# One queue for the first loads, three homes for raw weights and more idle products at the start of a fused RWKV-6 and MLP kernel

## The chip, the cores and the metric

The kernel runs on one core of a Trainium2 chip. Times are microseconds of device time for one execution; the kernel is called once with all its inputs in HBM and leaves its output in HBM. A shorter time is better.

The engines are called by the names of the profile: PE is TensorE (PEld its weight loads), DVE is VectorE, ACT is ScalarE, POOL is GpSimd and SP is SyncE, which here only issues DMA transfers.

## The reference

Two blocks, one after the other. The first is a linear recurrence over 768 time steps for 4 batches and 8 heads of 48 values; the second is a layer norm and an MLP with a residual.

```python
B, H, S, D = r.shape                      # 4, 8, 768, 48
state = zeros((B, H, D, D))
for t in range(S):
    kt, vt, rt, wt = k[:, :, t], v[:, :, t], r[:, :, t], w[:, :, t]
    cur = einsum('bhd,bhe->bhde', u[None] * kt, vt)
    y[:, :, t] = einsum('bhd,bhde->bhe', rt, state + cur)
    state = wt[..., None] * state + einsum('bhd,bhe->bhde', kt, vt)

x = y.transpose(0, 2, 1, 3).reshape(B, S, H * D)          # (4, 768, 384)
mu, var = mean(x), mean((x - mu) ** 2)                    # over the last axis
xn = (x - mu) / sqrt(var + 1e-6) * g_ln
out = x + maximum(xn @ w_ch1, 0) @ w_ch2                  # 384 -> 1536 -> 384
```

All inputs and the output are float32.

## The kernel before

The work is cut into eight rounds (4 batches, 2 halves of 384 time steps each), and each round into two units of four heads. Round `rnd` has the units `q = 2 * rnd` and `q = 2 * rnd + 1`; in the text "w0" or "k1" means the tile of w or k of unit 0 or 1 of round 0. Time is worked in chunks of 64 steps with six levels of doubling inside a chunk.

A round has a front and an MLP.

- The front (`front`, line 1165) loads w, k and r (`load`, line 350, tiles called `nat`), turns them with PE transposes into PSUM (`turn`, line 380: products `w_ps`, `k_ps`, `r_ps` with the identity) and copies them out on ACT (tiles `w`, `k`, `r`). `totals` (line 421) forms products of w over 2, 4, ... 64 steps (`tot`, `decay`). For each of the six levels `quads` (line 517) multiplies k by r on PE (PSUM tile `a`), `grow` (line 546) scales k and r in place by `tot` on DVE, and `keep` (line 567) writes the masked result to `A`. `own` (line 450) forms the term with u (tiles `rk`, `own_row`), `load_v` (line 649) and `own_term` (line 673, tile `vo`) bring in v, `states` and `outputs` (lines 688 and 752) form the state and the output of the round, `normalize` (line 813) does the layer norm (tile `xn`) and `turn_x` (line 865) turns its result (`xT_ps`, then `xf` on ACT).
- The MLP (`mlp`, line 1055) multiplies `xf` by the first weights (PSUM `h_ps`, in later rounds also `hd_ps`) and the result `h` by the second weights `w_sb` (PSUM `o`), adds the residual and stores.

The MLP weights come in as 24 tiles, called `raw`, of 128 by 384 values in 64-bit words that hold them (384 KB each). `convert` (line 926) fetches one (SP) and rebuilds float32 words from it with three ACT operations (`upper`, `lower`, `sign`) and two DVE operations (`shift`, `join`). The first twelve make the first weights (shown as `w` in the profile, next to the tile `w` of the front), the other twelve make `w_sb`. Later rounds, from round 1 on (`THREE`, line 339), split `xf` into a high and a low part and a difference, tiles `hl` and `xd`; these use the homes of `raw` as well.

**Order.** Nothing is ordered by hand. Each step is an operation of a planner (`Plan`, line 51) with an engine, a cost, the tiles it reads and writes, a priority `pri` (lower first) and, for a DMA, a latency `lat` and a `size` in microseconds of DMA time. `order` (line 104) simulates the engines and writes out one program order for each. A tile has a tag, and a tag has a number of homes, buffers that its tiles take in turn (`HOMES`, line 254). An operation that makes a tile starts, in the plan, when a home is free. DMA transfers are taken by the planner to follow one another: `dma = max(dma, t) + size`, and the data is there at `dma + lat`.

Instructions are then issued in that order on each engine[...].

**Idle products.** Where PE would stand for over 0.4 us before 90 us of planned time, `order` puts in products of zeros (`idle`, line 1241, PSUM tile `idle`), `n` of them with 128 columns each, up to three in one product. The planner's cost of one is 0.24 us, doubled for `t < 5.0`. PE counts as free from 1.0 us of planned time on, SP from 0.8, ACT from 0.9 (`busy`, line 1250).

**The first loads.** In round 0 `front` issues w, k and r of both units: unit 0's three on SP's queue, unit 1's three on ACT's queue, each one transfer of 288 KB; SP's queue then has the broadcast of u (`u_bc`, 192 KB), raw weights, v, and the loads of round 1.

Of the kernel before, what the change touches and what calls it, by code (L numbers as in the profile page):

```python
# [10 lines left out]
F32R = mybir.dt.float32r  # L11
# [39 lines left out]
class Plan:  # L51
# [52 lines left out]
    def order(self, busy, idle=None, until=0.0):  # L104
        ops = self.ops
        left, users, last = {}, {}, {}
        for op in ops:
            left[op.i] = len(op.need)
            for j in op.need:
                ops[j].next.append(op.i)  # L110
            for n in op.uses:
                users[n] = users.get(n, 0) + 1
        free = dict(busy)
        held = {"DVE": 0.0, "POOL": 0.0}
        portless = {"DVE": 0.0, "POOL": 0.0}
        ready = {e: [] for e in free}
        for op in ops:
            if not left[op.i]:
                for e in op.costs:
                    ready[e].append(op)  # L120
        dma, todo, out, tiled = 0.0, len(ops), [], False

        def start_of(op, e):
            t = max(free[e], op.ready)
            tags = [tag for tag, _ in op.new]
            for tag in set(tags):
                n = tags.count(tag)
                if len(self.homes[tag]) < n:
                    return None
                if tag not in self.dynamic and self.queue[tag][0] != op.i:  # L130
                    return None
                t = max(t, sorted(self.homes[tag])[n - 1][0])
            if op.port:
                t = max(t, held["POOL" if e == "DVE" else "DVE"])
                if e == "POOL" and t < op.ready + self.PATIENCE:

                    if portless["DVE"] - t < 0.6 * op.costs[e]:
                        t = max(t, free["DVE"] + 0.3)
            return t

        while todo:
            best = None
            for e, waiting in ready.items():
                at = [(t, op) for op in waiting if (t := start_of(op, e)) is not None]
                if not at:
                    continue
                first = min(t for t, _ in at)
                t, op = min(
                    ((t, op) for t, op in at if t <= first + self.WAIT[e]),
                    key=lambda x: (  # L150
                        x[1].pri + self.STAY * (e == "PE" and x[1].tiled != tiled), x[1].i
                    ),
                )
                if best is None or t < best[0]:
                    best = t, op, e
            assert best
            t, op, e = best
            if idle and e == "PE" and t < until and t - free["PE"] > 0.4 and self.homes[idle[0]]:
                n = int((t - free["PE"]) / (idle[1] * (2 if t < 5.0 else 1)))
                home = min(self.homes[idle[0]])  # L160
                if n and home[0] <= free["PE"]:
                    out.append((free["PE"], lambda n=n, home=home: idle[2](n, home[1])))
                    self.homes[idle[0]].remove(home)
                    self.homes[idle[0]].append((t, home[1]))
            if e == "PE" and op.tiled != tiled:
                tiled = op.tiled
                t += self.DRAIN[tiled]
            for x in op.costs:
                ready[x].remove(op)
            op.eng, op.start, cost = e, t, op.costs[e]  # L170
            free[e] = t + cost
            if e in held:
                (held if op.port else portless)[e] = t + cost
            op.end = t + cost + op.lat
            if op.size:
                dma = max(dma, t) + op.size
                op.end = max(op.end, dma + op.lat)
            for tag, name in op.new:
                home = min(self.homes[tag])
                self.homes[tag].remove(home)  # L180
                self.queue[tag].remove(op.i)
                self.place[name] = home[1]
            for n in op.uses:
                users[n] -= 1
                last[n] = max(last.get(n, 0.0), op.end)
                if not users[n]:
                    self.homes[self.tile_tag[n]].append((last[n] + self.HOP, self.place[n]))
            for j in op.next:
                nxt = ops[j]
                hop = self.HOP if set(nxt.costs) != {e} else 0.0  # L190
                nxt.ready = max(nxt.ready, op.end + hop)
                left[j] -= 1
                if not left[j]:
                    for x in nxt.costs:
                        ready[x].append(nxt)
            fn = op.fn
            out.append((t, fn if len(op.costs) == 1 else lambda fn=fn, e=e: fn(e)))
            todo -= 1
        return [fn for _, fn in out]
# [5 lines left out]
def kernel(  # L205
# [13 lines left out]
    PE, ACT, DVE, POOL, SP = (  # L219
        InOrder(tc, e) for e in (nc.tensor, nc.scalar, nc.vector, nc.gpsimd, nc.sync)  # L220
    )

    B, H, S, D = r.shape
    P = 128
# [5 lines left out]
    U = H // NH  # L230
    TT = 3
    RN = TT * P
# [21 lines left out]
    HOMES = {  # L254
        "nat": 5, "w": 1, "k": 2, "r": 2, "tot": 1, "decay": 3, "rk": 2, "own": 2, "own_row": 1,
        "v": 2, "vx": 2, "vo": 2, "s": 2, "last": 4, "rx": 2, "sx": 2, "x": 2, "xn": 3,
        "xf": 3, "stats": 2, "mv": 2, "rstd": 2, "raw": 4, "rest": 8, "h": 12, "w1": 4, "wl": 4,
    }
    plan = Plan(HOMES | {"a": 2, "b": 4}, ("a", "b"))
    tiles = {}  # L260

    def tile_(tag, name, shape, dtype=F32):
        if name in tiles:
            return tiles[name]
        if tag == "a":
            tiles[name] = a_homes[plan.place[name]]
            return tiles[name]
        if tag == "nat":
            tiles[name] = nat_homes[plan.place[name]]
            return tiles[name]  # L270
        pool = banks if tag == "b" else homes
        t = pool.tile(shape, dtype, tag=f"{tag}{plan.place[name]}", name=name)
        tiles[name] = t
        return t
# [9 lines left out]
    ROWS, ROW = 2, TT * D  # L284
# [62 lines left out]

    SRC = {"w": w, "k": k, "r": r}

    def load(nm, q, eng="SP", pri=None):  # L350
        b, f, g = units[q]
        name = f"nat_{nm}{q}"

        queue = SP if eng == "SP" else ACT

        def go():
            to = tile_("nat", name, None)
            if q // U < ROWS:
                queue.dma_start(
                    out=to[:, 0 : NH * ROW].rearrange("p (h x) -> p h x", h=NH),  # L360
                    in_=SRC[nm][b, ts(g, NH), ds(f * RN, RN)]
                    .rearrange("h (p c) d -> p h (c d)", p=P),
                )
                return
            for c in range(TT):
                queue.dma_start(
                    out=by_tile(to)[:, c, :, 0:D],
                    in_=SRC[nm][b, ts(g, NH), ds(f * RN + c * P, P)].rearrange("h p d -> p h d"),
                )

        if pri is None:
            pri = at(q // U, "wrk".index(nm))
        new = [] if nm == "r" and q in both_units else [("nat", name)]
        cost, size = (0.5, 0.8) if q // U < ROWS else (1.65, 1.2)
        plan.add(eng, cost, go, w=[name], new=new, pri=pri, lat=2.0, size=size)

    def by_tile(t):
        return t.rearrange("p (c h d) -> p c h d", c=TT, h=NH)
# [486 lines left out]
    def turn_x(rnd, kc):  # L865
        ps, xf, pri = f"xT_ps{rnd}_{kc}", f"xf{rnd}_{kc}", at(rnd, 28)
# [12 lines left out]
        hl, xd = f"xhl{rnd}_{kc}", f"xd{rnd}" if kc < 2 else f"xd2{rnd}"  # L879
        new = [("b", ps), ("xf", xf)]  # L880
        if rnd >= THREE:
            new += [("raw", xd)] if kc == 0 else [("rest", xd)] if kc == 2 else []
            new += [("raw", hl)]
        plan.add(
            "PE", 0.33, go, r=[f"xn{rnd}_{i}" for i in range(TT)], w=[ps], new=new,
            pri=pri, lat=0.17,
# [4 lines left out]

        def high():
            if kc < 2:
                tile_("raw", xd, [P, 2, RN], F32R)
            else:
                tile_("rest", xd, [P, RN], F32R)
            tile_("raw", hl, [P, 2, RN], F32R)
            ACT.activation(out=x_parts(rnd, kc)[0], in_=tiles[xf], func=AF.Copy, scale=TOP)
# [266 lines left out]
    def front(rnd):  # L1165
        qs = [U * rnd + g for g in both_units]
        if rnd:
            for q in qs:
                load("w", q)
                load("k", q)  # L1170
        else:
            for i, nm in enumerate("wkr"):
                for q, eng in zip(qs, ("SP", "ACT")):
                    load(nm, q, eng, i)
        if rnd == 0:
            plan.add(
                "SP", 0.6, lambda: SP.dma_start(
# [105 lines left out]
```

## Time and profile before

| what | us |
|---|---|
| median of 7 runs | 556.52 |
| lowest and highest of the 7 | 553.68, 564.84 |
| the profiled execution's own time | 554.24 |
| its span in the profile | 552.5 |
| PE busy in it | 534.4 (97%) |
| DVE busy | 360.0 (65%) |
| ACT busy | 254.6 (46%) |

How to read the lines shown later: an instruction's row names the engine, the operation and its tiles as out<-in, without buffer numbers. "L40" stands in every row, because each instruction is recorded in one helper at that line, so instructions are told apart by their tiles. The chain that ended last is followed back from the last instruction: at each step to what released it, or to the instruction before it on its engine. In a timeline, brackets give the idle time of the engine before the row and what ended it. A product in float32 appears as two instructions, a transpose as one. Idle products count as busy time of PE.

### The profile page before, as it was taken

To read this page: it belongs to the slowest core of one execution; us is meant where nothing else is said; L and a number is where in the kernel's file an instruction comes from. 1 tells how busy PE (TensorE), PEld (TensorE's weight loads), DVE (VectorE), ACT (ScalarE), POOL (GpSimd) and SP (SyncE) were. 2 spreads that over 40 slices of the span, in tenths; PEclk is the share of its full clock that TensorE was granted. 3 is DMA by queue.
4 is the path that set the end of the run, shared out by engine and by line. 5 is a ranking of instruction groups with operands and counts; after the bars stand their busy time and mean duration, and the time that the engine had idled before them with its cause. 6 is when DMAs were issued, how large, how long until landed. Compare 5 with 4: busy or idle time off the path is not lost.

```text
span 552.5 us, 20001 instructions
## 1 busy us (share of the span) xinstructions
PE 534.4 (97%) x8820; PEld 414.2 (75%) x8820; DVE 360.0 (65%) x719; ACT 254.6 (46%) x555; POOL 71.4 (13%) x93
## 2 busy tenths in 40 slices
PE   8998998999999899999999999999999999999997
PEld 7876566666888676889758986798668867967964
DVE  5899999889999876688815987186635422531300
ACT  4788886643384360654605544153245412521500
POOL 7034013371213210011000100000001000000000
PEclk9999999999999999999999999999999999999999
DMA  9975873278534533266005530234003302301101
GB/s 278 260 189 116 247 180 69 74 148 220 146 68 96 139 66 71 68 144 162 30 15 134 105 97 17 70 74 127 17 30 96 110 14 72 112 34 61 40 0 43
DMA packets 118838, 55.80 MB, mean 101 GB/s; under 512 B 86880, under 2 KB 115680, under 8 KB 118752
## 3 DMA queue, kind: packets, MB, share of 16 engines
q1 hardware_dynamic: 117168, 53.65, 38.1%
q8 instruction: 69, 1.13, 0.9%
q10 hardware_dynamic: 1584, 0.88, 0.5%
q14 instruction: 17, 0.14, 0.1%
HBM read 45.05 MB, written 7.10 MB: 94 GB/s over the span
## 4 chain that ended last, share of the span: by engine, by line
PE 86%; DVE 4%; DMA 4%; issue 3%; SPq 1%; ACT 1%; POOL 0%; DVEq 0%; POOLq 0%
PE o L40 33%; PE h_ps L40 17%; PE a L40 17%; PE hd_ps L40 7%; PE w_ps L40 3%; PE k_ps L40 2%; PE r_ps L40 2%; PE kn_ps L40 2%; PE idle L40 2%; DVE A L40 1%; PE xT_ps L40 1%; SPq L40 1%; DMA nat<-in_w_dram 1%; DVE r L40 1%; DVE k L40 1%
## 5 line engine op out<-in xcount | busy, mean ns | idle before, releaser
L40 PE MATMUL o<-w_sb,h 128*128 128x384 f32 x576 | 196.4, 491 | 0.0
L40 PEld LDWEIGHTS o<-w_sb,h 128*128 128x128 f32 x576 | 106.9, 190 | 64.5 <-issue 0.3
L40 ACT COPY h<-hd_ps 128x384 f32<-128x384 f32 x84 | 39.9, 479 | 97.4 <-PE hd_ps L40 96.0
L40 PEld LDWEIGHTS a<-r,k 48*32 48x32 f32 (+5 forms) x4608 | 63.4, 126 | 23.8 <-issue 11.1
L40 DVE SCALAR_TENSOR_TENSOR h<-h_ps,h 128x384 f32<-128x384 f32 x84 | 46.5, 557 | 51.4 <-PE h_ps L40 49.9
L40 ACT ACTIVATE h<-h 128x384 f32<-128x384 f32 x84 | 43.8, 525 | 71.3 <-DVE h L40 70.9
L40 PE MATMUL a<-r,k 48*32 48x32 f32 (+5 forms) x4608 | 69.6, 212 | 6.7 <-issue 4.2
L40 DVE TENSOR_TENSOR x<-o,x 128x384 f32<-128x384 f32 x24 | 13.4, 557 | 79.1 <-PE o L40 79.1
L40 PE MATMUL h_ps<-xhl,wl 128*128 128x384 f32 x252 | 62.4, 356 | 0.0
L40 PE MATMUL h_ps<-xhl,wh 128*128 128x384 f32 x252 | 57.7, 337 | 0.0
L40 PE MATMUL hd_ps<-xd,d 128*128 128x384 f32 x252 | 56.4, 353 | 0.0
L40 DVE TENSOR_TENSOR k<-k,tot 112x768 f32<-112x768 f32 (+1 forms) x45 | 41.2, 915 | 21.9 <-PE a L40 15.8
L40 PEld LDWEIGHTS h_ps<-xhl,wl 128*128 128x128 f32 x252 | 44.1, 188 | 3.3 <-ACT r L40 0.2
L40 PEld LDWEIGHTS h_ps<-xhl,wh 128*128 128x128 f32 x252 | 45.2, 188 | 0.0
L40 PEld LDWEIGHTS hd_ps<-xd,d 128*128 128x128 f32 x252 | 43.2, 188 | 2.6
L40 DVE TENSOR_TENSOR r<-r,tot 112x768 f32<-112x768 f32 (+1 forms) x45 | 41.3, 917 | 0.0
L40 DVE COPY_PREDICATED A<-mask,a 128x768 f32<-128x768 int8 x32 | 38.4, 1207 | 2.5 <-PE a L40 2.5
L40 POOL TENSOR_TENSOR vo<-v,own 128x576 f32<-128x576 f32 x11 | 16.3, 1483 | 152.1 <-DVE x L40 136.7
L40 POOL TENSOR_TENSOR rk<-nat,nat 128x576 f32<-128x576 f32 x11 | 17.5, 1595 | 110.3 <-DMA nat<-in_r_dram 48.3
L40 ACT COPY A<-a 32x384 f32<-32x384 f32 x32 | 15.0, 468 | 27.5 <-PE a L40 27.2
L40 PE MATMUL a<-v,A 64*64 64x48 f32 x384 | 24.4, 221 | 2.7 <-issue 1.2
L40 PEld LDWEIGHTS a<-v,A 64*64 64x64 f32 x384 | 21.2, 133 | 6.9 <-issue 3.5
(94 smaller groups left out, 758.7 us busy)
## 6 DMA issues: line engine op xcount, KB each, us to landing
d<-w1d SPq DMA_DIRECT2D x84, 192.0 KB, 2.5
raw<-in_moe_w_ch_dram SPq DMA_DIRECT2D x24, 384.0 KB, 4.3
v<-in_v_dram SPq DMA_DIRECT2D x48, 96.0 KB, 3.0
out_dram<-x SPq DMA_DIRECT2D x24, 192.0 KB, 1.9
nat<-in_w_dram SPq DMA_DIRECT2D x36, 96.0 KB, 3.0
nat<-in_k_dram SPq DMA_DIRECT2D x36, 96.0 KB, 3.6
nat<-in_r_dram SPq DMA_DIRECT2D x36, 96.0 KB, 2.9
vx<-v SPq DMA_DIRECT2D x32, 72.0 KB, 3.2
```

Of the source, the lines that this page charges most:

```text
L40: return lambda *args, **kw: self.tc.keep_in_program_order(f(*args, **kw))
```

## The change

There are five edits.

- `load` has no engine any more: every load of w, k and r is issued by SP. In round 0 the six loads go in the order w0, w1, k0, r0, k1, r1 with priorities 0, 0.5, 1, 1.5, 2, 2.5, ahead of u's broadcast (priority 5) and of the raw weights (14 and up).
- The planner's figures for a load of w, k or r become 2.2 for the latency (all rounds) and 0.95 for the size (rounds 0 and 1).
- The tag `raw` has three homes instead of four.
- The tile `xd` (kc 0 and 1) has a tag and a home of its own, of the size of one raw home.
- The planner takes 1.78 times 0.24 us instead of 2 times 0.24 for an idle product that is placed before 5.0 us.

```diff
-                n = int((t - free["PE"]) / (idle[1] * (2 if t < 5.0 else 1)))
+                n = int((t - free["PE"]) / (idle[1] * (1.78 if t < 5.0 else 1)))
...
-        "xf": 3, "stats": 2, "mv": 2, "rstd": 2, "raw": 4, "rest": 8, "h": 12, "w1": 4, "wl": 4,
+        "xf": 3, "stats": 2, "mv": 2, "rstd": 2, "raw": 3, "xd": 1, "rest": 8, "h": 12, "w1": 4, "wl": 4,
...
-    def load(nm, q, eng="SP", pri=None):
+    def load(nm, q, pri=None):
...
-        queue = SP if eng == "SP" else ACT
...
-                queue.dma_start(
+                SP.dma_start(
...
-        cost, size = (0.5, 0.8) if q // U < ROWS else (1.65, 1.2)
-        plan.add(eng, cost, go, w=[name], new=new, pri=pri, lat=2.0, size=size)
+        cost, size = (0.5, 0.95) if q // U < ROWS else (1.65, 1.2)
+        plan.add("SP", cost, go, w=[name], new=new, pri=pri, lat=2.2, size=size)
...
-            new += [("raw", xd)] if kc == 0 else [("rest", xd)] if kc == 2 else []
+            new += [("xd", xd)] if kc == 0 else [("rest", xd)] if kc == 2 else []
             new += [("raw", hl)]
...
-                tile_("raw", xd, [P, 2, RN], F32R)
+                tile_("xd", xd, [P, 2, RN], F32R)
...
-            for i, nm in enumerate("wkr"):
-                for q, eng in zip(qs, ("SP", "ACT")):
-                    load(nm, q, eng, i)
+            for i, (nm, q) in enumerate((("w", 0), ("w", 1), ("k", 0), ("r", 0), ("k", 1), ("r", 1))):
+                load(nm, q, i / 2)
```

More of the change, by code (lines that the diff above doesn't have):

```diff
@@ L365, in go @@
             for c in range(TT):
-                queue.dma_start(
+                SP.dma_start(
                     out=by_tile(to)[:, c, :, 0:D],
```

## The prediction

> **What bounds the kernel now.** I read the engine shares first, then the chain that ended last, then the opening microseconds as a timeline, then who waits for whom.
>
> The shares (engine, busy us, share of the span, instructions):
>
> ```profile
> PE 534.4 (97%) x8820; PEld 414.2 (75%) x8820; DVE 360.0 (65%) x719; ACT 254.6 (46%) x555; POOL 71.4 (13%) x93
> ```
>
> PE is the bound, but the figure counts idle products too. The table by stretches splits the span (us, then busy us of PE, PEld, DVE, ACT, POOL, clock, DMA share, GB/s):
>
> ```profile
> 15.00:60.00 45.00, 41.78 (x1090) 32.19 (x1088) 40.87 (x91) 37.55 (x80) 10.99 (x11) 1.00 0.76 198
> 60.00:90.00 30.00, 27.85 (x470) 18.89 (x469) 27.05 (x43) 24.13 (x53) 6.45 (x5) 1.00 0.77 185
> 90.00:552.50 462.50, 451.62 (x7190) 351.84 (x7188) 283.00 (x572) 186.33 (x412) 44.22 (x41) 1.00 0.32 81
> ```
>
> From 90 us on PE has 11 us of holes in 462, and nothing in this change adds or removes a product there. Up to about 57 us, where round 0's MLP begins, PE waits for a serial front: 5.4 us of idle products before 30 us and 9.5 us between 30 and 60. DVE is busy 40.9 of 45 us there. So the span is "when the front of round 0 is finished" plus a nearly solid block of products. A microsecond taken off the front comes off the end, unless another wait takes its place.
>
> The chain at its beginning (start us, us, what):
>
> ```profile
> 0.81 3.42 DMA nat<-in_w_dram
> 4.22 0.14 issue
> 4.36 5.34 PE w_ps L40 x24
> 9.70 1.07 PE k_ps L40 x6
> 10.77 0.66 PE r_ps L40 x6
> 11.42 1.97 PE k_ps L40 x18
> 13.38 1.97 PE r_ps L40 x18
> 15.35 1.51 PE a L40 x96
> ```
>
> Six transposes take 5.34/4 = 1.33 us for w, then 1.07, then 0.66: from about 10.45 us on PE runs the same instruction twice as fast. One k_ps product's duration falls from 418 ns to 272 ns at that point. The granted-clock column says 1.00 throughout, so it doesn't show this. PE's first instructions by time:
>
> ```profile
> 0.99 2.50 PE L40 MATMUL idle<-nought 128*128 128x384 f32 x4 [0.99 <-DVE eps L40]
> 4.36 5.34 PE L40 MATMUL w_ps<-ident,nat 128*112 128x128 f32 x24 [0.87 <-DMA nat<-in_w_dram]
> ```
>
> Idle products ran from 0.99 to 3.49, then PE stood 0.87 us until the first w tile landed.
>
> [...] between 3 and 4 us the ACT queue had 69% and the SP queue 43% of the engines' time, while w of unit 0 was still unfinished. [...]
>
> **The change, part by part.**
>
> *One queue.* ACT loses three DMA issues (0.42, 0.52, 0.53 us), made at 1.00 to 2.54 when it had only a table load and a square root; its first copy comes at 5.89, so this gives nothing; POOL issues no transfer. SP gains three of about 0.55 us: u_bc's issue moves from 2.40 to about 4.05, the first raw weight from 3.13 to 4.75, v from 8.37 to 9 to 10. All of these have slack: ACT first touches a raw weight at 15.76 and v is first read near 39. u_bc is needed at 13.65, which becomes about 11.8; behind six loads of 0.295 MB at the 350 GB/s of the 3 to 6 us stretch it ends near 2.5 + 1.97/0.35 = 8.1. Cost 0; if u_bc came as late as 13, DVE would stand 1 us and lose half of the gain. The w tile of unit 0 no longer shares: 0.16 MB had moved by 3.0, the other 0.135 takes 0.39 at 350 GB/s[...]: 3.6 instead of 4.22. The others follow every 0.84 us: w1 4.5, k0 5.3, r0 6.2, k1 7.0, r1 7.9.
>
> *Idle products.* The planner's w arrives at 0.8 + 0.95 + 2.2 + 0.1 hop = 4.05 instead of 0.8 + 0.8 + 2.0 + 0.1 = 3.7. With PE free at 1.0, n = int(3.05/(0.24 × 1.78)) = 7 columns of 128 instead of int(2.7/0.48) = 5. Five took 2.50 us with the last one's latency, (2.50 - 0.36)/5 = 0.43 each. Seven end their issue at 0.99 + 7 × 0.43 = 4.0. PE then has w (landed 3.6) without a hole, and starts 0.36 us sooner. If w still landed at 4.22, the hole is about 0.2 us and the start is unchanged.
>
> *Clock.* [...] Transposes from 4.0: (7.04 - 4.0)/0.222 = 13.7 slow ones, the other 58.3 at 0.1095 = 6.4 us, ready at 13.43 instead of 15.35. Gain **1.9 us**. [...] Low end 0 if the array isn't released by zero products[...]. The loads stay ahead: w1's transposes start at 6.7, k0's at 8.3, r0's at 9.6, all over 2 us after landing.
>
> *What follows.* DVE's chain starts with `tot<-w` at 10.24, after the fourth copy of w. Copies now end near 8.8; DVE does 4.9 us of products (to 13.7) and meets the first `k<-k,w` at 14.4 instead of 16.31. From there DVE is nearly solid, so the 1.9 us is carried to `xf` at 56.22, where the MLP begins.
>
> *Three raw homes.* Before, four weights are fetched at once; ACT holds one for about 0.54 + 2 × 0.60 = 1.74 us. No ACT wait on a raw transfer appears in the list of waits. With three, the fourth load waits for ACT's first conversion. One home turns in 0.45 issue + landing + 1.74; landing is 5.3 us at the median of the first 40 us and 3.6 from 40 to 90. Three homes thus give one weight in (0.45 + 5.3 + 1.74)/3 = 2.5 us, later 1.93. The kernel uses twelve in 15.8 to 54.6 (3.2 each) and twelve in 54.4 to 85 (2.5 each). I take 0: between 85 and the last `o` group that needs w2 (about 101) lie 16 us. Bounds: from -1 (fewer early weights leave ACT and DVE to the front) to +6, the rival below.
>
> *A home for xd.* Same bytes: four homes of 3,072 per partition before, three and one now. The hl tiles of one round are all released by the same last h_ps product, with xd just earlier, so nobody waits longer. 0.
>
> *New order.* The planner recomputes every engine's order from the new latencies. That is a real uncertainty. The visible piece is here:
>
> ```profile
> 44.06 3.89 DVE L40 TENSOR_TENSOR vo<-v,own 128x576 f32<-128x576 f32 x1
> 47.88 0.54 DVE L40 CUSTOM_DVE_ANT_0 w<-w,held 128x768 uint16<-128x768 uint16 x1
> ```
>
> The same vo takes 0.75 elsewhere; POOL was in rk from 43.00 to 47.34. 3.1 us of DVE's chain stand still.
>
> **Sum.** -0.36 - 1.5 + 0 + 0 = -1.9 us. The profiled execution took 554.24 (span 552.5 and 1.74 around it), so 552.3 against itself. The median of the seven is 556.52, 2.3 higher; the gain applied to that gives 554.6, and I give the number on the median's footing.
>
> **Rivals.**
>
> *A, head start alone: 42%, 554.6, own range 553.0 to 556.2.* For it: DVE's solid front, PE's solid rest.
>
> *B, head start and the block goes: 30%.* If the new order parts rk and vo, 1.9 + 3.1 = 5.0, so 551.5. For it: before, chip time lags the plan by 3.7 us at the first level (15.35 against 3.7 + 72 × 0.11 = 11.6 by the planner's costs), so operations meant to be apart can meet; now 13.43 stands against 12.0. Against: POOL and DVE lag together.
>
> *C, no earlier release: 10%, 556.2.* [...] w may land late and reopen the hole. [...]
>
> *D, raw weights arrive late: 18%, 559.1 to 561.4.* [...] The planner takes 1.05 + 2.0 = 3.05 us for a raw load; landing was 5.3 early. With four homes the extra load ahead hid the 2.25 us difference; with three, an ACT conversion can stand in front of copies that free PSUM, and SP's next loads of k and r stand behind a raw load that waits for its home. Two or three stands of 2.25 us on the front, 4.5 to 6.8, on top of 554.6. It decides once landings of raw loads stay over 3 × 2.53 - 0.45 - 1.74 = 5.4 us. For it: 5.3 is close to that. Against: traffic falls after 40 us, and SP's longest wait on ACT's release was 2.7.
>
> **How the numbers follow.** A measurement of this kernel tells about 0.5% from no change, 2.8 us: the bands end at 553.7 and 559.3. A puts 13 points below and 29 within; B 28 below, 2 within; C 2 below, 8 within; D 2 within, 16 above. Faster 43%, same 41%, slower 16%. The range 549.8 to 559.2 leaves out the far end of B and most of D.
>
> **What will show it.** The page after should have PE without a hole from 1.0 us, the first w_ps at 3.9 to 4.1, transposes falling to 109 ns at or before 7.8, and the first `a` at 13 to 14. `tot<-w` should start near 8.8 and `xf` near 54.3. An ACT row waiting for the raw transfers, or k_ps or r_ps waiting for their loads by over 1 us, means D. A vo on DVE of 0.75 in round 0 means B. I am wrong if the first `a` comes at 13.4 and `xf` still at 56: then the front is held by a transfer or a conversion that I call hidden.

## The result and the profile after

The changed kernel takes **562.27 us** at the median (556.39 to 566.50) against 556.29 for the kernel before on the same chips: a ratio of **1.0095, interval 1.0073 to 1.0116**, so 0.95% slower. The ratios leave out the executions that lie over 1.5% above the fastest of their kernel, so they aren't the quotients of the medians. The forecast was 554.6 with a range up to 559.2. The profiled execution took 559.89 (before: 554.24), its span 557.8 (before: 552.5): 5.3 us longer, close to what the medians say.

The page's line of engine shares, after (engine, busy us, share of the span, instructions):

```profile
PE 538.7 (97%) x8828; PEld 417.8 (75%) x8828; DVE 358.9 (64%) x719; ACT 254.6 (46%) x555; POOL 76.6 (14%) x93
```

PE is busy 4.3 us longer, with eight instructions more. The same stretches as before (us, then busy us of PE, PEld, DVE, ACT, POOL, clock, DMA share, GB/s):

```profile
15.00:60.00 45.00, 39.71 (x990) 31.66 (x990) 37.55 (x85) 33.17 (x71) 10.16 (x10) 0.96 0.77 191
60.00:90.00 30.00, 28.61 (x456) 18.93 (x455) 27.14 (x50) 24.99 (x53) 5.72 (x3) 1.00 0.78 191
90.00:557.80 467.80, 456.34 (x7208) 355.10 (x7207) 285.20 (x573) 187.57 (x415) 49.23 (x43) 0.99 0.32 81
```

Two things stand out. The front between 15 and 60 has lost: DVE is busy 37.55 us of it where it was busy 40.87. And from 90 us on, PE is busy 456.34 where it was 451.62, for 18 instructions more, at a clock of 0.99 instead of 1.00: the same work takes 4.7 us more busy time, while the holes (467.80 - 456.34 = 11.46 us, before 10.88) hardly grew.

**The head start came.** The chain of waits at its beginning, after (start us, us, what):

```profile
0.99 3.36 PE idle L40 x6
4.34 3.27 PE w_ps L40 x24
...
12.86 1.51 PE a L40 x96
14.37 0.63 PE idle L40 x2
15.00 0.80 PE a L40 x45
15.80 0.78 issue
16.59 0.70 PE a L40 x36
17.29 5.72 DMA nat<-in_w_dram
```

PE goes from the idle products to w_ps without a hole, the transposes of w take 3.27 us instead of 5.34, and the first level group `a` begins at 12.86 instead of 15.35, 2.5 us earlier.

**It was spent by 40 us.** To follow useful work, I count every product of PE except the idle ones at what it takes at full clock in the trace (497.6 us in total, in all these kernels). That is working on the trace, not a view of it, and good to within a microsecond:

| done by (us) | 15 | 20 | 30 | 40 | 57 | 85 | 100 | 200 | 400 |
|---|---|---|---|---|---|---|---|---|---|
| before | 7.8 | 10.9 | 18.5 | 26.8 | 33.4 | 59.5 | 72.8 | 160.6 | 352.9 |
| after | 9.4 | 11.3 | 19.3 | 26.8 | 32.5 | 57.5 | 67.4 | 155.2 | 347.6 |

The lead of 1.6 us is 0 at 40 us; the changed kernel is 2.0 behind at 85 and 5.4 behind at 100, and stays there to the end. So there are two questions: what ate the lead, and what happened between 85 and 100 us.

**What happened between 85 and 100.** The chain of waits of the changed kernel there:

```profile
86.79 2.52 PE a L40 x175
89.31 2.24 issue
91.54 0.66 PE a L40 x17
92.20 6.82 PE h_ps L40 x12
```

In the middle of a run of level products PE stands for 2.24 us, and the profile names no releaser ("issue": the engine waited for nothing that the profile shows). Then twelve h_ps products take 6.82 us; the same twelve take 3.87 at 63.46 in the same trace. The windows view of 90 to 105 us, first the kernel before, then the changed one; the clock is the last column but two:

```profile
90.00:105.00 15.00, 14.75 (x284) 9.57 (x283) 13.51 (x24) 12.36 (x29) 1.75 (x2) 1.00 0.16 43
```

```profile
90.00:105.00 15.00, 12.87 (x149) 7.58 (x152) 9.40 (x12) 7.00 (x17) 4.88 (x3) 0.77 0.06 16
```

The clock falls from 1.00 to 0.77, and 149 products of PE stand in the window in place of 284 (not the same ones, so the counts show less than the clock). The trace's clock record has PE at half speed from 90.90 to 97.72, and also from 39.70 to 43.11 and from 169.40 to 176.23: 17.06 us in all, 3.41 in the kernel before. Each stretch begins 1.6 to 4.5 us after the start of a long hole: at 89.31 (2.24), at 35.23 (2.05) and at 167.4 (2.33). The last of the three holes is of another kind and is taken up below. The hole at 35.23 as the chain shows it:

```profile
34.24 0.99 PE a L40 x82
35.23 2.05 issue
37.28 0.25 PE a L40 x4
```

**What the "issue" holes are.** The page's table of DMA queues has this row after the change (packets, MB, share of the engines):

```profile
q8 instruction: 69, 1.13, 0.9%
```

1.13 MB in 69 packets is 16 KB each, and PE's program has 17,780 instructions in the trace (a weight load and a product counted apart, with some 120 for semaphores): 258 for each packet. With exactly 256 instructions more, in g1 and g4 below, the row has 70 packets. These packets are PE's own program arriving. I numbered PE's instructions from 0 in the order of the trace and took, in the fourteen kernels of this case, every place inside a run of products of the same tiles, written to `a`, where over 0.7 us pass from the start of one instruction to the start of the next. There are 60, and **all 60 stand at number 193 of a block of 256**.

At each of the 60 places PE waited for the packet of the very next block. From the moment PE crosses one border to the moment it can start the block after the next border, these holes took 2.3 to 6.3 us, 4.0 at the median. At the medians, 1.4 us pass until the packet starts, 1.1 for the packet itself and 1.4 from its end to the next instruction. That last step is nearly constant, 1.1 to 1.6 us, and at none of the 958 borders of the fourteen traces did PE go on earlier than 1.09 us after the end of the packet.

A level group (96 products, 192 instructions with their weight loads) takes 1.5 us, so a whole block of such products is used up in some 2.0 us (an estimate: 256/192 of 1.5). Where level groups follow each other and fill a block, PE is through before the next block is there, and stands. In the trace of the changed kernel over 0.7 us pass at 7 of the 69 borders, all 7 of them behind a product written to `a`; none of the 12 borders behind one of the wider products, written to `h_ps` or `o`, is among them.

**The hole at 167.40.** Here PE waited for DVE, whose k and r took 2.12 and 2.15 us while POOL worked on rk, as in the prediction vo took 3.89 beside rk and 0.75 elsewhere:

```profile
165.50 2.12 DVE L40 TENSOR_TENSOR k<-k,tot 112x768 f32<-112x768 f32 x1
167.53 2.15 DVE L40 TENSOR_TENSOR r<-r,tot 112x768 f32<-112x768 f32 x1
165.38 1.42 POOL L40 TENSOR_TENSOR rk<-nat,nat 128x576 f32<-128x576 f32 x1 [1.64 <-DMA nat<-in_r_dram]
166.88 1.99 POOL L40 TENSOR_TENSOR rk<-rk,u_bc 128x576 f32<-128x576 f32 x1
```

In g4, which has the same order of DVE and POOL, DVE came first there and took 0.95 for each of the two, and no such hole follows. So of the 8.5 us that half clock cost in this execution (half of 17.06), 5.1 lie behind holes at a border and 3.4 behind this one.

### The profile page after: what moved, and what is told of

Same layout as the page of the kernel before. It is cut to its first block, busy times and chain, and to the rows that moved or that the text cites. A ratio compares the mean times of both kernels' runs of the same rounds, so it can differ in the third digit from the quotient of the medians.

```text
span 557.8 us, 20010 instructions
## 1 busy us (share of the span) xinstructions
PE 538.7 (97%) x8828; PEld 417.8 (75%) x8828; DVE 358.9 (64%) x719; ACT 254.6 (46%) x555; POOL 76.6 (14%) x93
## 3 DMA queue, kind: packets, MB, share of 16 engines
q8 instruction: 69, 1.13, 0.9%
## 4 chain that ended last, share of the span: by engine, by line
PE 89%; DVE 4%; DMA 3%; issue 2%; ACT 1%; SPq 1%
PE o L40 32%; PE h_ps L40 20%; PE a L40 17%; PE hd_ps L40 8%; PE r_ps L40 2%; PE w_ps L40 2%; PE k_ps L40 2%; PE kn_ps L40 2%; PE idle L40 1%; PE xT_ps L40 1%; DMA nat<-in_w_dram 1%; DVE r L40 1%; DMA nat<-in_k_dram 1%; DMA w1d<-w1diff 1%; DVE k L40 1%
## 5 line engine op out<-in xcount | busy, mean ns | idle before, releaser
L40 PE MATMUL hd_ps<-xd,d 128*128 128x384 f32 x252 | 57.7, 357 | 0.0
L40 POOL TENSOR_TENSOR vo<-v,own 128x576 f32<-128x576 f32 x9 | 12.0, 1334 | 168.2 <-DVE x L40 141.6
L40 POOL TENSOR_TENSOR rk<-nat,nat 128x576 f32<-128x576 f32 x12 | 21.5, 1788 | 69.7 <-DMA nat<-in_r_dram 45.6
L40 PE MATMUL h_ps<-xf,w 128*128 128x384 f32 x72 | 27.7, 532 | 0.0
```

The lines of the kernel that those rows point to most:

```text
L40: return lambda *args, **kw: self.tc.keep_in_program_order(f(*args, **kw))
```

## The experiments

The table holds all of them. The ratio is to the kernel before on the same chips, with its interval. "Clock loss" is (1 - granted clock) times the span, averaged over the compared runs, and "rest" is the mean time less that. "a, issue" is the idle time ahead of level products with no releaser, from one profiled execution of each (the row of the level products among the costliest groups; none is given for e2). The row of before holds the runs beside g1 to g4; its clock loss was 2.5 beside e1 to e4 and 3.5 beside f1 to f4, so a difference of 1 us in that column says nothing.

| kernel | ratio | clock loss us | rest us | a, issue us |
|---|---|---|---|---|
| before | 1 | 3.0 | 553.1 | 4.2 |
| after | 1.0095 [1.0073, 1.0116] | 7.9 | 553.3 | 7.2 |
| e1 head only | 1.0035 [1.0006, 1.0063] | 5.3 | 552.8 | 3.3 |
| e2 order only | 1.0096 [1.0068, 1.0125] | 8.7 | 553.0 | – |
| e3 three raw homes only | 1.0018 [0.9989, 1.0048] | 3.2 | 554.3 | 2.5 |
| e4 after, four raw homes | 1.0005 [0.9968, 1.0043] | 2.5 | 554.1 | 5.6 |
| f1 after, +100 instructions | 1.0027 [1.0002, 1.0052] | 6.7 | 552.1 | 6.0 |
| f2 before, +64 instructions | 1.0166 [1.0129, 1.0203] | 8.7 | 557.4 | 7.2 |
| f3 full head, before's order | 1.0013 [0.9988, 1.0039] | 4.3 | 553.4 | 5.9 |
| f4 e4, +80 instructions | 0.9977 [0.9958, 0.9995] | 3.0 | 552.7 | 2.6 |
| g1 before, +256 instructions | 0.9974 [0.9938, 1.0011] | 3.2 | 553.3 | 5.7 |
| g2 before, +172 instructions | 0.9972 [0.9947, 0.9997] | 2.4 | 552.2 | 3.8 |
| g3 full head, +172 | 0.9974 [0.9951, 0.9997] | 3.2 | 551.5 | 5.7 |
| g4 after, +256 instructions | 1.0075 [1.0047, 1.0103] | 7.8 | 553.5 | 7.5 |

Before and after differ by 4.9 us in clock loss and by 0.2 in the rest. Over the 51 runs of the kernel before that were compared with e1 to e4, time against clock loss has a slope of 0.85 and a correlation of 0.84. Nearly the whole loss of the changed kernel is PE's clock.

### The change taken apart

Theory 1: the head start is real, and the recomputed order loses it in longer holes and half clock. Theory 2: the head start can't reach the end, because transfers hold the front. Theory 3: one queue for all loads costs by itself. D is the rival of the prediction, raw weights that come late.

**e1_head_only**: the order of the kernel before, its loads all on SP, seven idle columns at the start.

```diff
-                n = int((t - free["PE"]) / (idle[1] * (2 if t < 5.0 else 1)))
+                n = 7 if t < 5.0 else int((t - free["PE"]) / idle[1])
...
-        queue = SP if eng == "SP" else ACT
+        queue = SP
```

> The kernel before with every engine's order as it was; only the six first loads all go out on SP's queue and the idle products ahead of the first transposes are 7 columns of 128 instead of 5. Theory 1 (the head start is real, and the recomputed order loses it again in longer holes of PE and the half clock after them): PE at full clock by 7.8 us, the first level products at 12.8 to 13.5 instead of 15.35, and 1.5 to 2.5 us less than before in the end. Theory 2 (a head start can't reach the end, because the front waits for transfers): full clock as early, but the same time as before within 0.5 us. Theory 3 (one queue for the loads is itself what costs): slower than before by 2 us or more.

**e2_order_only**: the changed kernel's order, its first loads on two queues again, five idle columns.

```diff
-                n = int((t - free["PE"]) / (idle[1] * (1.78 if t < 5.0 else 1)))
+                n = 5 if t < 5.0 else int((t - free["PE"]) / idle[1])
...
-                SP.dma_start(
+                (ACT if q == 1 else SP).dma_start(
```

> The changed kernel with every engine's order as it has it, but unit 1's first loads back on ACT's queue and 5 columns of idle products instead of 7. Theory 1: the order alone costs, so this is slower than the changed kernel by 1.5 to 2.5 us (the head start gone), 6.5 to 8 us over before. Theory 3: this is back at the time of before.

**e3_raw3_only**: the kernel before with the two edits of `raw` and `xd` (three homes and one), nothing else.

> The kernel before with three homes for raw weights and one for xd; first loads, latencies and idle products as before. The planner recomputes the order. Rival D of the prediction (raw weights late) says 3 to 5 us slower than before, with ACT waits on the raw transfers of 0.5 us and more. Theory 1 says that any recomputed order is a new draw of holes: within 5 us of before on either side, and told by the length of PE's holes of over 1.5 us and by the mean clock, not by the raw transfers.

**e4_queue_raw4**: the changed kernel with those two edits undone; the planner's order follows.

> The changed kernel with four homes for raw weights, shared with xd as before. Rival D says that it takes back 3 to 5 us of the loss and that the ACT waits on raw transfers go. Theory 1 says that the waits on raw transfers go or shrink, but that the time follows the holes of PE and the clock after them.

Measured: e2 lies on the changed kernel (1.0096 against 1.0095), though it has neither the queue nor the idle columns; so the new order, with the three homes that it was made for, carries the loss. Theory 1 was right in this and wrong in its number: without the head start e2 should have been 1.5 to 2.5 us slower than the changed kernel, and it is level with it. e1 missed its forecast too. Theory 1 expected 1.5 to 2.5 us less than before, and it lost 0.35%; its first level group came at 14.47 in its trace, not at 12.8 to 13.5, after a wait of 0.96 us at 8.8 for the load of r. That loss is close to the 2 us that theory 3 asks for; f3 below, with the same loads on one queue in a better order, lies at 1.0013 and gives theory 3 no support. e3 is level, where D expected 3 to 5 us: three homes with the order of the planner for them cost nothing that can be told. e4 is level too, and this looked like D, since one home more took the loss away. The waits for raw weights that D needs are there in the changed kernel, in ACT's timeline:

```profile
25.62 0.56 ACT L40 ACTIVATE w<-raw 128x384 f32<-128x384 f32 x1 [1.12 <-DMA raw<-in_moe_w_ch_dram]
89.08 0.56 ACT L40 ACTIVATE w_sb<-raw 128x384 f32<-128x384 f32 x1 [1.04 <-DMA raw<-in_moe_w_ch_dram]
```

But e3 has the three homes without the loss, and the planner's order differs between before, after, e3 and e4, so other instructions lie at the borders of the blocks. The next runs keep each order and move only the borders.

### The borders moved

Theory 4: PE's holes stand where two dense level groups lie in one block of 256 instructions, and what an edit does to the time depends on what it moves across these borders. Idle products are a handle on that: a stretch of `n` columns can be issued as products of up to three columns, of one, or of half of one, with more instructions and little more time on PE (busy for 14.9 us in 40 idle instructions before, 15.1 in 72 in f2, 16.8 in 168 in g1; weight loads are not counted).

**f1_after_split, f2_before_split, f4_queue_raw4_split**: in some stretches, products of one column at most. The lists are (0, 1, 2, 4, 5, 7) for f1, (1, 7) for f2, (3, 5, 6) for f4. The lines are f2's.

```diff
+        most = 1 if len(calls) in (1, 7) else TT
+        calls.append(n)
...
-            now = min(n, TT)
+            now = min(n, most)
```

> The changed kernel with the same order on every engine and the same amount of idle products; in six of its eight idle stretches they are cut into products of 128 columns instead of up to 384, which adds 100 PE instructions before 55 us and no other work. Theory 4 (PE's holes in the middle of a group of small products stand where one block of 256 of its instructions ends, and their length is how much faster than 3.2 to 5.3 us PE used up the block before): the holes stay at instruction 193 of each 256 and so fall on other products. From the changed kernel's own trace, with 3.7 us for a block, the shortfalls add up to 8.5 us instead of 14.3, and what is over 1 us in each to 0.3 instead of 4.6. So less half clock: clock loss 3 us instead of 8.3, and 554 to 557 instead of 562. Theory 1 in its first form (the holes belong to the order, to what a product waits for): holes at the same products as in the changed kernel, and the same time within 1 us.

> The kernel before with the same order and the same amount of idle products; in its second and eighth idle stretch they are cut into products of 128 columns, 64 PE instructions more. Theory 4: shortfalls of 13.8 us instead of 8.5, over 1 us each 4.8 instead of 2.0: clock loss 7 to 9 us instead of 3.5, and 3 to 6 us slower than before, though nothing of the change is in it. Theory 1 in its first form: the same as before within 1 us.

> The changed kernel with four raw homes again (as in the run with that alone), and idle products cut in three stretches, 80 PE instructions more. Theory 4: shortfalls 7.7 us instead of 11.4, over 1 us each 1.2 instead of 3.2; that run stood level with before, so this is 2 to 4 us faster than before.

**f3_head2**: e1 with the first six loads in the changed kernel's order w0, w1, k0, r0, k1, r1, so that the whole head start is there ahead of the order of before.

> The kernel before in its own order, with the changed kernel's head in full: six first loads on SP in the order w0, w1, k0, r0, k1, r1 and 7 columns of idle products (4 more PE instructions). If the head start can be carried by the order of before: PE useful work 1.5 to 2 us ahead of before at 15 us and still over 1 us at 60, and 1 to 2 us less at the end. If it is absorbed: ahead at 15 us, level with before by 40 us, and the same time within 1 us.

Measured: f1 takes 0.7 of the 0.95% away from the changed kernel without touching its order, its queue or its homes; between 90 and 105 us it has no hole and no half clock:

```profile
90.00:105.00 15.00, 15.00 (x416) 10.29 (x408) 13.27 (x21) 11.13 (x26) 6.03 (x3) 1.00 0.34 88
```

f2 costs the kernel before 1.66%, more than all of the change, by 64 idle instructions. f4 gains 0.23%. All three signs came out as theory 4 expected, and all three sizes missed. f1 has a median of 558.3 where 554 to 557 was expected, and its clock loss is 6.7 where 3 was: other holes at borders brought half clock elsewhere (from 17.72, 147.42 and 307.85). f4 is 1.3 us faster than before, not 2 to 4. f2 is about 9 us slower, not 3 to 6: its clock loss of 8.7 fits, but its rest is 4.3 longer as well. A part of that is neither a hole of PE at a border nor its clock. DVE's vo took 4.98 us beside POOL's rk, 1.1 more than the 3.89 of the kernel before:

```profile
44.60 4.98 DVE L40 TENSOR_TENSOR vo<-v,own 128x576 f32<-128x576 f32 x1
44.63 1.41 POOL L40 TENSOR_TENSOR rk<-nat,nat 128x576 f32<-128x576 f32 x1
46.19 2.78 POOL L40 TENSOR_TENSOR rk<-rk,u_bc 128x576 f32<-128x576 f32 x2
```

f3 is level with before (1.0013), the case of a lead that is absorbed: its first level group begins at 12.37, and by 20 us its useful work is 10.9, that of the kernel before. A hole of 1.1 at 15.6 and half clock from 18.11 to 21.52 took the whole 1.9 us.

Two objections to these runs remain: cutting idle products might change the time by itself, for better or worse. The last four runs answer them. If only the borders matter, exactly 256 instructions more must leave every later border on the product where it was.

**g1_before_256, g2_before_172, g3_head2_172, g4_after_256**: each stretch of idle products is left (0), cut to one column (1) or to half a column, 64 by 64 (2).

```diff
+        cut = (0, 1, 1, 0, 2, 2, 2, 2, 2)[len(calls)]
+        most, wide = (TT, P) if cut == 0 else (1, P // cut)
+        n *= P // wide
...
-                t[:, 0 : now * P], zeros, nought.broadcast_to([P, now * P]), start=True, stop=True
+                t[0:wide, 0 : now * wide], nought.broadcast_to([P, wide]),
+                nought.broadcast_to([P, now * wide]), start=True, stop=True,
```

That is g1; g2 has (0, 0, 1, 0, 1, 0, 0, 2, 0), g3 (0, 0, 2, 0, 1, 0, 2, 1, 2), g4 (0, 0, 1, 0, 2, 1, 2, 1).

> Theory 4: PE's instructions arrive in blocks of 256, and holes stand where two dense level groups lie in one block. The kernel before, every product of value in its old order, with idle products of 30 to 57 us cut finer so that exactly 256 instructions are added before 57 us. One whole block more leaves every later border at the product where it was. Theory 4 expects the holes after 57 us at the products of the kernel before (the fourth and sixth level group near 85 and 111 us, and near 187 us) and a time within 0.4% of before, 555.5 to 559.5, although four times as many instructions are added as the 64 of the second stretch that cost 1.7%. The rival, that the cut itself or the number of instructions costs, expects more than those 9 us, 566 or above.

> The changed kernel with exactly 256 instructions added before 57 us by finer idle products. Theory 4: borders after 57 us stand at the products where the changed kernel had them, so the holes near 89 and 167 us come back and the time is within 0.4% of the changed kernel, +0.6 to +1.3% against before, where 100 added instructions gave +0.27%. The rival, that finer idle products help by themselves [...], expects +0.3% or less.

> Theory 4: the kernel before with 172 instructions added in four stretches of idle products. A sum of (3.7 us minus the time that PE takes for a block) over all blocks falls from 8.5 to 6.8, the part over 1 us each from 2.0 to 0.3. So holes are short and the clock is kept: clock loss 2 to 4 us instead of about 4, time 1 to 3 us under before, 554 to 556. The rival, that cutting costs by the number of instructions, expects at least the loss of the 64 instructions, 566 or above.

> The kernel before's order with the six first loads on one queue and seven idle columns, with 172 instructions added in idle stretches. Theory 4: head start kept (first level group near 12.8) and the border sum 6.7 (0.3) instead of 8.8 (1.9): 1 to 3 us under the uncut head start kernel, 553 to 556. If the head start can't be kept whatever the borders (rival: front held by a transfer), it equals the kernel with 172 instructions and no head start.

Measured: g1 with 256 instructions more lies level with the kernel before (0.9974, the interval includes 1), where 64 cost 1.66%. g4 with 256 more keeps most of the changed kernel's loss (1.0075), where 100 took most of it away; the intervals of g4 and f1 just overlap, between 1.0047 and 1.0052. The holes came back to their products. PE's instruction numbers at the holes after 57 us were 3265, 4289 and 7873 in the kernel before and are 3521, 4545 and 8129 in g1, each 256 further; 3265, 4801, 7361 and 10433 in the changed kernel became 3521, 5057, 7617 and 10689 in g4, which has two more, at 6849 and 7105. The other forecast for g4 failed: the hole near 167 us, that behind POOL, didn't come back. Taken over the 60 borders that follow the added instructions, the gaps of g1 go with those of the kernel before (correlation 0.89) and those of g4 with the changed kernel's (0.87). For f2 against before it is 0.28, and for f1 against after 0.00.

The chain of the kernel before, that of g1, then that of g4 (this last is the hole at 89.31 of the changed kernel, after the same 175 products):

```profile
82.89 2.80 PE a L40 x189
85.69 1.49 issue
87.18 0.30 PE a L40 x3
```

```profile
85.33 2.82 PE a L40 x189
88.16 2.21 issue
90.36 0.29 PE a L40 x3
```

```profile
91.33 2.52 PE a L40 x175
93.85 2.19 issue
96.04 0.43 PE a L40 x17
96.47 4.07 PE h_ps L40 x12
```

g4 also shows that a hole of that length doesn't always bring half clock: here h_ps takes 4.07 right after it, and the half clock came elsewhere in that execution (from 39.93, 135.50 and 186.70), each time behind a hole at a border (2.12 us at 36.79, 1.54 at 133.09, 1.15 at 185.33).

g2 and g3 were chosen for the fewest crowded blocks, and lie 0.28% and 0.26% under before, as forecast, both with an interval that just leaves out 1. With f4 they have the lowest times found. But g1, which should stand level with before, has the same 0.9974 as g3, so a gain of some 1.5 us isn't safely told from none. And g3 with the head start ends level with g2 without it, which is what the rival of a front that can't keep a head start had foretold.

## Why the prediction was wrong

Two steps of it failed: that the lead is carried through the front to `xf`, and that the new order is worth 0. What stands in their place are holes of PE at the borders of its program's blocks, and the half clock behind long holes.

**The head start: right.** Idle products without a hole from 0.99 (the line is in the chain above), w_ps from 4.14 (forecast 3.9 to 4.1), PE at full clock from 5.56 by the trace's record (forecast 7.04), `tot<-w` at 8.17 (forecast 8.8), first `a` at 12.8 (forecast 13.43). The 7.04 and the 1.5 us in the prediction's sum were my estimates, not shown by the trace of before; what sets the moment of that switch isn't shown in these traces. It differs between them, and the 2.5 us of these two owe something to luck: the kernel before had the latest switch of all the traces, at 10.41. In the seven traces with the full head start the first `a` comes at 12.37 to 13.59, in the six with the old one at 13.72 to 15.28 (e1, with half of it, is left out). The medians are 12.8 and 14.65: 1.9 us apart, as forecast. Rival C falls with that.

**"The 1.9 us is carried to xf": this step failed.** `xf` began at 58.03, not at 54.3 and not even at the 56.22 of before. The prediction itself named this outcome as the sign of a front held by a transfer or a conversion. One transfer took a part: PE waited 1.23 us for a load of w of round 1.

```profile
23.15 0.84 PE L40 MATMUL w_ps<-ident,nat 128*112 128x128 f32 x6 [1.23 <-DMA nat<-in_w_dram]
```

That load was issued at 17.29, after 8.5 us of issues of v on SP's queue, and took 5.72 to land. Holes at borders stand in the same stretch, of 0.78 us at 15.80 and 2.05 at 35.23, and the half clock from 39.70 to 43.11, worth 1.7 where PE sets the pace. The new order also left DVE idle for 2.22 us before its first `k<-k,w`, since the products of `rk` and `own_row` had been put behind it. But f3, with the order of before, lost its lead as fully by 20 us without either of them, in a hole at a block's border and the half clock after it. How much each of these took from the changed kernel's front isn't measured apart. I called DVE's chain solid at 40.9 of 45 us; PE's own program was the other limit, and the shares don't name it.

**"From 90 us on PE has 11 us of holes in 462, and nothing in this change adds or removes a product there": true of products, wrong in what it was used for.** The holes stayed at 11 us, the products stayed, and the stretch still took longer, because the clock fell to half behind single long holes. The hole of 2.24 us at 89.31 and the 6.83 us at half clock behind it cost 2.2 + 3.4 = 5.6 us by themselves. The kernel before has a hole of 1.49 at the same instruction number and keeps its clock there; the changed kernel loses 3.4 us against it between 85 and 100.

**"New order. 0": this was the term that decided.** I let the order be uncertain and priced only the one block that it might remove, `rk` beside `vo`. That block did go:

```profile
49.16 1.42 DVE L40 TENSOR_TENSOR vo<-v,own 128x576 f32<-128x576 f32 x2
```

Two vo products in 1.42 us, where one had taken 3.89: B's mechanism happened, and its 3.1 us didn't reach the end. A part of it came back at once: DVE's `w<-w,held`, 0.54 us in the lines of the prediction, took 2.33 at 40.96, while POOL was in rk from 41.47 to 42.88. Later the same kind of block made the hole at 167.40. The other side of the term, what a new order may add, had no number. It should have had one: the kernel before shows "issue" rows with no releaser, 2.27 us at the longest, and a clock of 0.97 between 150 and 200 us right behind that hole. e2 shows what the new order costs with the homes that go with it (+0.96%), and f2 how far borders alone, with the blocks of DVE that follow, can take a kernel: +1.66% for 64 instructions that do nothing.

**One queue and raw homes at 0.** f3 (1.0013) and e3 (1.0018) bear these out within their intervals. For D, ACT's waits for raw weights did come (2.7 us in three places), but the loss doesn't follow them: f1 keeps the three homes, waits 6.9 us in six places and loses 0.27%; e3 keeps them, waits 3.4 us in two places and loses nothing that can be told. That these waits cost nothing at all within the changed kernel isn't shown.

**What stays open.** Why a border shows at number 193 of 256 in the trace's count isn't settled, nor what starts the transfer of a block: at the 60 holes it began from 0.2 us before the border to 3.2 us after it, at other borders up to 7 us before. Whether the head start would pay in a kernel free of these holes isn't either. g3 has it and g2 hasn't, and they end level; but in their traces the first `a` lies only 1.0 us apart (13.6 and 14.6), and g3 still lost 2.4 us in two holes before 24 us. Its `xf` comes at 58.91 against 55.74 in g2; yet their spans are 553.8 and 553.3. f1's comes at 61.53, 3.5 us later than the changed kernel's, and its span is 1.0 shorter. So my "a microsecond taken off the front comes off the end" is in doubt as well. The changed order's last 0.27% in f1 has no cause shown. Why f1 keeps a clock loss of 6.7 us while its rest falls by 1.2 isn't shown either.

## What to carry to other kernels

When many small products follow each other on PE, number its instructions: a pause with no releaser that always falls on the same number modulo 256 was the program arriving here, and an edit of the order or of the count can move it (against before, the gaps' correlation fell to 0.28 in f2 with 64 instructions more), so in a kernel like this a difference of 1% between two orders says nothing yet about the edit's idea. Before crediting or blaming an edit, run it once more with the borders moved (some dozens of harmless instructions) and once with exactly 256 added as a control. And price a long hole on PE at its length plus half of the slow clock that may follow, not at its length alone.

## What was not expected of the hardware

- At the 60 holes the next 256 instructions were there 2.3 to 6.3 us after the border before, 4.0 at the median, while a level group of 192 instructions runs in 1.5 us. So dense small products outrun their own program.
- Half clock followed single holes of 2.05 to 2.33 us in the changed kernel, for 3.41 or 6.83 us each. In f1 one of 0.86 us at 15.55 was followed by half clock from 17.72 to 21.13, while one of 2.19 in g4 was not.
- 64 idle instructions in 17,700 changed a kernel by 1.66%, and 256 of them by nothing that can be told.
- Two DVE products that take 0.95 us each in g4 took 2.12 and 2.15 beside POOL's rk, and the hole of 2.33 us that this made in PE was followed by 6.83 us at half clock.
